# The values of two head pairs: reordered by TensorE transposes instead of a trip through DRAM

## The chip, the core and the metric

The kernel runs on one core of a Trainium2 chip. A core has a matrix engine (TensorE, PE in the profile, with its weight loads listed apart as PEld), a vector engine (VectorE, DVE), a scalar engine (ScalarE, ACT), a general engine (GpSimd, POOL) and a sync engine (SyncE, SP) that here only issues DMA transfers. Each engine works through its own list of instructions in the order in which they were written, and waits on semaphores for the others. PE reads SBUF and writes PSUM, whose eight banks are its scarce resource. The metric is the device time of one execution in microseconds (us).

## What is computed

Attention over blocks comes first, and a bilinear feed-forward layer behind it. The inputs q, k and v are of shape (4, 8, 768, 64): batch, head, position, head dimension. A small 8x8 matrix for each head is normalised by rows and columns five times and then mixes the 8 blocks of k and of v:

```python
P = sort_net                     # (4, 8, 8, 8), normalised five times
k_sorted = einsum('bhij,bhjcd->bhicd', P, k_b)      # blocks of 96 positions
v_sorted = einsum('bhij,bhjcd->bhicd', P, v_b)
scores = q_b @ k_sorted^T / 8                       # inside each block
out    = softmax(scores) @ v_sorted                 # (4, 8, 768, 64)
x = out as (3072, 512)
y = ((x @ w_a) * (x @ w_b)) @ w_out                 # w_a, w_b: 512x1536
```

## The kernel before

**Tiling.** Heads are worked in pairs: batch `b` has pairs `p` = 0 to 3, called (b, p) below. The two heads of a pair lie side by side in the 128 partitions. The feed-forward layer takes one batch at a time, in two halves of 384 positions. Batch 0 uses plain products (`ab_plain`, line 749), batches 1 to 3 a scheme with fewer products over sums of the operands (`ab_strassen`, line 831), and `out_plain` (line 899) multiplies by `w_out`.

**Order.** Every piece of work is an `Op` with an assumed duration, the pieces it depends on, the buffers it takes and gives back, and a rank. `Plan.solve` (line 132) simulates the engines with these assumed durations, picks at each step the piece that can start first (ties by rank), and writes the whole program in that order. So the order on every engine is fixed when the program is built; if a transfer takes longer on the chip than assumed, the engine that needs it waits at that place. Assumed latencies are in the table `LAT`, line 39. If one piece's cost or resources change, the order of all that follows may change a little.

**Stages.** Attention of batch 0 is done first, in half pairs. Then the feed-forward products of batch 0 run on PE (lines 954 to 956) with the attention of batch 1 (lines 958 and 959) put between them, one pair after about three of the 24 products. While this goes on, POOL issues the loads of batch 2 (line 952) and forms sums of weights (`w_sums`, line 769) for the later scheme.

**Values of one pair, by the two routes.** The function `attention` (line 721) calls `q_part`, `mix_part` and `so_part`.

- Through DRAM, where `VDMA(b, p)` is true: `v_tok` (line 534, its products at 537) mixes the pair with 2 products of 384 columns; DVE copies the result from PSUM to the tile `vm`, as 128 x 768 numbers (`v_tok_copy`, line 540, shown under line 250 of the helper `copy`); SP writes `vm` to a DRAM tile `vd` (`v_out`, issue at line 546), waits until this has landed, and reads it back in another order into the tile `vs` (`v_back`, issue at line 550).
- On the chip, where `VDMA` is false: `mix_pe` (line 484, products at 489) mixes with 12 products of 128 columns, so that positions lie along the free dimension; `mix_copy` (line 523) moves the result to the tile `vT`; `v_pe` (line 554, at 559) makes 8 transposes of 128x128, one for each block; `v_copy` (line 562) moves 96 x 1024 numbers to `vs`. The attention of batch 0 uses these steps too, in halves (12 products at line 500, 4 transposes, copies of half the size).

In both routes `o_pe` (line 589, products at 593) multiplies the exponentials `eT` with `vs`, 16 products for a pair. The order of the positions inside a block must be the same for k and v, so `mix_copy` for k writes `kT` in the order that the flag `tc_o` gives; the number of elements is the same. q has its own order and does not depend on the flag.

Buffers: `vs` has 4 slots, `vT` 4, `vm` 2, `v2` (v as loaded) 6. Each pair takes one route only.

In the listing, `sp_dma` adds two pieces: the issue on SP and the transfer. `load` adds a POOL issue and a transfer.

Of the kernel before, what the change touches and what calls it, by code (L numbers as in the profile page):

```python
# [35 lines left out]
class Plan:  # L36
# [12 lines left out]
    def add(self, eng, dur, fn, deps=(), get=(), put=(), rank=0.0, lat=None):  # L49
        alts = dict(eng) if isinstance(eng, (list, tuple)) else {eng: dur}  # L50
        op = Op(alts, fn, deps, list(get), list(put), rank, lat, len(self.ops))
        for key in op.put:
            self.holders[key] = self.holders.get(key, 0) + 1
        self.ops.append(op)
        return op
# [136 lines left out]
STRASSEN_AB = (1, 2, 3)  # L192
STRASSEN_OUT = ()
QDMA = lambda b, p: b >= 3
VDMA = lambda b, p: b >= 1


@with_exitstack
def kernel(
# [284 lines left out]
    def mix_pe(b, p, what):  # L484
        src = buf((what + "2", b, p))
        mix = buf((what + "m", b, p))
        for c in range(NCH):
            for e in range(2):
                nc.tensor.matmul(  # L489
                    mix[e * D:(e + 1) * D, c // 4, c % 4 * P:(c % 4 + 1) * P],  # L490
                    lhsT=src[:, e, c * D:(c + 1) * D],
                    rhs=s_all[:, b * H + 2 * p + e], start=True, stop=True)
# [136 lines left out]
    def mix_part(b, p, rk, split):  # L629

        pair = ("pair",)
        tc_o = VDMA(b, p)
        km = add("PE", 0.46, lambda: mix_pe(b, p, "k"), [k_in[b, p], s_ok[b, p]],
                 get=[("pair", ("km", b, p))], put=[("k2", b, p)], rank=rk)
        ks = []
        for h in ((0, 1) if split else (None,)):
            ks.append(add("ACT", 0.48 if split else 0.8,
                          lambda h=h: mix_copy("ACT", b, p, "k", h, tc_o), [km, o_pads] + ks,
                          get=[("kT", ("kT", b, p))] if not ks else [], put=[("km", b, p)],
                          rank=rk + (0.3 if h == 1 else 0)))  # L640
        if tc_o:
            vm = add("PE", 0.33, lambda: v_tok(b, p), [v_in[b, p], s_ok[b, p]],
                     get=[("pair", ("vm", b, p))], put=[("v2", b, p)], rank=rk)
            vc = add("DVE", 0.95, lambda: v_tok_copy("DVE", b, p), [vm],
                     get=[("vm", ("vb", b, p))], put=[("vm", b, p)], rank=rk)
            vo = sp_dma(0.35, 0.6, lambda: v_out(b, p), [vc], put=[("vb", b, p)], rank=rk)
            vb = sp_dma(0.35, 0.9, lambda: v_back(b, p), [vo, o_pads],
                        get=[("vs", ("vs", b, p))], rank=rk)
            return ks, [vb]
        vm = add("PE", 0.46, lambda: mix_pe(b, p, "v"), [v_in[b, p], s_ok[b, p]],  # L650
                 get=[("pair", ("vm", b, p))], put=[("v2", b, p)], rank=rk + 0.05)
        vs = []
        for h in ((0, 1) if split else (None,)):
            alts = (("DVE", 0.56), ("ACT", 0.48)) if split else (("DVE", 0.95), ("ACT", 0.8))
            op = add(alts, None, None, [vm, o_pads] + vs,
                     get=[("vT", ("vT", b, p))] if not vs else [], put=[("vm", b, p)],
                     rank=rk + (0.3 if h == 1 else 0.05))
            op.fn = lambda h=h, op=op: mix_copy(op.eng, b, p, "v", h, tc_o)
            vs.append(op)
        return ks, vs  # L660
# [20 lines left out]
    def v_part(b, p, h, vsrc, rk):  # L681

        pe = add("PE", 0.28 if h is not None else 0.5, lambda: v_pe(b, p, h), [vsrc, o_ident],
                 get=[("bank", ("vp", b, p, h))], put=[("vT", b, p)], rank=rk)
        alts = (("ACT", 0.6), ("DVE", 0.42)) if h is not None else (("ACT", 1.0), ("DVE", 0.69))
        op = add(alts, None, None, [pe, o_pads, first.get(("v", b, p))],
                 get=[("vs", ("vs", b, p))] if h in (0, None) else [],
                 put=[("vp", b, p, h)], rank=rk)
        first["v", b, p] = op
        op.fn = lambda: v_copy(op.eng, b, p, h)  # L690
        return op
# [29 lines left out]
    def attention(b, p, rk):  # L721
        qd = q_part(b, p, None, rk)
        ks, vs = mix_part(b, p, rk, False)
        if not VDMA(b, p):
            vs = [v_part(b, p, None, vs[0], rk)]
# [337 lines left out]
```

## Time and profile before

| what | value |
|---|---|
| median of 3 runs | 253.11 us (252.26 to 253.12) |
| the profiled execution | 253.12 us |
| its span, first to last instruction | 251.3 us |
| around the span | 1.8 us |
| mean granted TensorE clock | 0.986 |
| PE busy | 237.3 us, 94% of the span |
| DVE busy | 154.4 us, 61% |
| ACT busy | 123.1 us, 49% |
| POOL busy | 115.0 us, 46% |
| issues of `vd` and of `vs` on SP | 12 each, 192 KB each |

Columns as in the profile: "x16" is a number of instructions; a row of the chain of work that ended last has its start, its duration (both in us), and what it was; a row of the DMA issues has the size of one and the time in us from issue to landing; a row of stretches has the busy time of each engine in turn (PE, PEld, DVE, ACT, POOL), then the granted clock, the mean busy share of the 16 DMA engines, and GB/s. `ps` is a tile in PSUM.

### The profile page before, as it was taken

The numbers are of one execution on the slowest core, as the hardware profiler recorded it, in microseconds if no ns is written. First come the engines' busy times: TensorE is split into PE (matmuls) and PEld (weight loads), VectorE is DVE, ScalarE is ACT, GpSimd is POOL, SyncE is SP. The second block draws the span as 40 slices with busy tenths as digits, with TensorE's granted clock in tenths as the row PEclk, the third lists the DMA queues.
The fourth block names the chain that finished last, engine by engine and source line by source line (L and its number), as shares of the span: only waits on it lengthen the run. The fifth ranks groups of instructions, "written<-read, shape, count | busy, mean of one in ns | idle before, by whom it ended". The sixth has DMA issues, their size and how long they took to land.

```text
span 251.3 us, 5639 instructions
## 1 busy us (share of the span) xinstructions
PE 237.3 (94%) x2168; PEld 132.3 (53%) x2168; DVE 154.4 (61%) x355; ACT 123.1 (49%) x239; POOL 115.0 (46%) x127
## 2 busy tenths in 40 slices
PE   7898999993799999999999999999999999999992
PEld 2466766651456445456654445555554455565440
DVE  6656654651348446689889453889885149787120
ACT  3366656453165621576654354867741147664110
POOL 8879999999940002009955110036250004445000
PEclk9999999999589999999999999999999999999999
DMA  5999999999971875534999986600033550000135
GB/s 70 176 202 180 203 202 182 168 202 209 156 136 37 148 195 107 129 87 63 144 142 135 126 205 176 147 3 0 0 65 72 121 120 4 1 0 0 44 83 125
DMA packets 51962, 28.68 MB, mean 114 GB/s; under 512 B 30432, under 2 KB 48864, under 8 KB 51936
## 3 DMA queue, kind: packets, MB, share of 16 engines
q0 software_dynamic: 24112, 14.16, 42.1%
q1 hardware_dynamic: 27824, 14.17, 26.6%
q8 instruction: 17, 0.28, 0.4%
q14 instruction: 9, 0.07, 0.1%
HBM read 30.68 MB, written 8.65 MB: 156 GB/s over the span
## 4 chain that ended last, share of the span: by engine, by line
PE 90%; DMA 5%; POOL 2%; ACT 1%; issue 1%; DVE 0%
PE ps L831 33%; PE ps L899 25%; PE ps L749 13%; PE ps L593 4%; PE ps L578 3%; DMA vs<-vd 3%; DMA q<-in_q_dram 2%; PE ps L473 2%; PE ps L537 2%; PE ps L489 2%; PE ps L500 2%; PE ps L983 1%; PE ps L559 1%; PE ps L612 1%; POOL k L362 1%
## 5 line engine op out<-in xcount | busy, mean ns | idle before, releaser
L306 POOL TENSOR_TENSOR hT<-a,f 128x384 bf16<-128x384 bf16 x34 | 31.1, 920 | 82.0 <-DVE f L306 81.0
L899 PE MATMUL ps<-w_out_sb,hT 128*128 128x512 bf16 x288 | 65.9, 379 | 0.0
L840 ACT COPY f<-ps 128x384 f32<-128x384 f32 x108 | 48.3, 481 | 22.7 <-PE ps L831 18.4
L899 PEld LDWEIGHTS <-hT 128*128 128x128 bf16 x288 | 27.0, 98 | 30.5
L306 DVE TENSOR_TENSOR f<-f,ps 128x384 f32<-128x384 f32 x54 | 29.1, 548 | 6.4 <-PE ps L831 5.0
L306 DVE TENSOR_TENSOR a<-f,ps 128x384 bf16<-128x384 f32 x54 | 29.5, 549 | 5.6 <-PE ps L831 4.2
L306 DVE TENSOR_TENSOR hT<-a,ps 128x384 bf16<-128x384 bf16 x42 | 23.1, 550 | 14.3 <-PE ps L749 7.4
L583 ACT ACTIVATE eT<-ps 96x768 bf16<-96x768 f32 x32 | 25.5, 807 | 11.0 <-PE ps L578 10.6
L248 ACT COPY o<-ps 128x512 f32<-128x512 f32 x14 | 8.1, 585 | 34.7 <-PE ps L899 31.6
L831 PE MATMUL ps<-tx,ws_b 128*128 128x384 bf16 x108 | 25.0, 326 | 0.0
L831 PE MATMUL ps<-tx,ws_a 128*128 128x384 bf16 x108 | 24.7, 327 | 0.0
L755 ACT CAST a<-ps 128x384 bf16<-128x384 f32 x24 | 11.5, 479 | 23.3 <-PE ps L749 19.8
L604 DVE TENSOR_TENSOR xp<-ps,rec 96x512 bf16<-96x512 f32 x32 | 21.5, 680 | 0.4
L250 DVE COPY o<-ps 128x512 f32<-128x512 f32 x10 | 6.9, 690 | 22.4 <-PE ps L899 22.4
L749 PE MATMUL ps<-xT,w_b_sb 128*128 128x384 bf16 x96 | 20.5, 337 | 0.0
L749 PE MATMUL ps<-xT,w_a_sb 128*128 128x384 bf16 x96 | 20.2, 335 | 0.0
L250 DVE CAST vm<-ps 128x768 bf16<-128x768 f32 x12 | 11.5, 956 | 12.3 <-PE ps L537 7.3
L831 PEld LDWEIGHTS <-ws_a 128*128 128x128 bf16 x144 | 13.4, 98 | 10.3 <-ACT f L840 1.6
L831 PEld LDWEIGHTS <-ws_b 128*128 128x128 bf16 x144 | 13.4, 98 | 9.7 <-ACT f L840 1.1
L248 ACT CAST kT<-ps 128x768 bf16<-128x768 f32 (+1 forms) x17 | 11.9, 705 | 13.3 <-PE ps L489 12.2
L593 PE MATMUL ps<-vs,eT 96*128 96x66 bf16 x256 | 12.7, 197 | 5.9 <-DMA vs<-vd 5.9
L831 PE MATMUL ps<-xT,w_b_sb 128*128 128x384 bf16 x72 | 17.4, 326 | 0.1
(88 smaller groups left out, 342.5 us busy)
## 6 DMA issues: line engine op xcount, KB each, us to landing
out_dram<-o SPq DMA_DIRECT2D x48, 128.0 KB, 2.4
k<-in_k_dram POOLq DMA_DIRECT2D x16, 192.0 KB, 5.9
v<-in_v_dram POOLq DMA_DIRECT2D x16, 192.0 KB, 6.2
vd<-vm SPq DMA_DIRECT2D x12, 192.0 KB, 2.4
vs<-vd SPq DMA_DIRECT2D x12, 192.0 KB, 3.2
q<-in_q_dram POOLq DMA_DIRECT2D x16, 96.0 KB, 7.2
w_a_sb<-in_moe_w_a_dram POOLq DMA_DIRECT2D x4, 384.0 KB, 7.3
w_b_sb<-in_moe_w_b_dram POOLq DMA_DIRECT2D x4, 384.0 KB, 8.6
```

The lines of the kernel that those rows point to most:

```text
L248: nc.scalar.copy(out=out, in_=in_)
L250: eng.tensor_copy(out=out, in_=in_)
L306: ENG[eng].tensor_tensor(out=out, in0=in0, in1=in1, op=op)
L578: nc.tensor.matmul(sc[:, e, i * BLK:(i + 1) * BLK], lhsT=kT[e * D:(e + 1) * D, at:at + P], rhs=rhs, start=True, stop=True)
L583: nc.scalar.activation(out=buf(("eT", b, p, h))[:, :, 0:HB], in_=buf(("sc", b, p, h))[0:BLK, :, 0:HB], func=AF.Exp, scale=float(scale))
L593: nc.tensor.matmul(ops_[:, e, i * OW:(i + 1) * OW], lhsT=eT[:, e, i * BLK:i * BLK + P], rhs=vs[:, h * NBH + i, e * OW:(e + 1) * OW], start ...
L604: nc.vector.tensor_tensor(out=_ap(xp, h * NBH * 2 * D, [[NB * 2 * D, BLK], [D, 2], [2 * D, NBH], [1, D]]), in0=_ap(ops_, 2, [[1024, BLK], ...
L749: nc.tensor.matmul(pf[:, 0:HW], lhsT=w_sb[:, kc, m * P:(m + 1) * P], rhs=buf(("xT", b))[:, kc, t * HW:(t + 1) * HW], start=(kc == 0), stop ...
L755: ea = add("ACT", 0.48, lambda: nc.scalar.copy(out=buf(("a", b, t, m)), in_=buf(("pf", b, t, m, "a"))[:, 0:HW]), [pa], get=[("a", ("a", b, ...
L831: nc.tensor.matmul(buf(key)[:, 0:HW], lhsT=lf(j), rhs=rf(j), start=start and j == 0, stop=j == 1, skip_group_check=not start)
L840: return add("ACT", 0.48, lambda: nc.scalar.copy(out=buf((name, b, g, n)), in_=buf(kA)[:, 0:HW]), [dep], get=[("f", (name, b, g, n))], rank=r)
L899: nc.tensor.matmul(po, lhsT=hT[:, t * 2 + m // G, m % G, c * P:(c + 1) * P], rhs=w_out_sb[:, m, :], start=(m == 0), stop=(m == KO - 1), sk ...
```

## The change

```diff
 QDMA = lambda b, p: b >= 3
-VDMA = lambda b, p: b >= 1
+VDMA = lambda b, p: 4 * b + p >= 6
```

`4 * b + p` counts the pairs from 0 to 15. Before, pairs 4 to 15 (all of batches 1, 2 and 3) went through DRAM. Now pairs 6 to 15 do, and pairs 4 and 5, that is (1,0) and (1,1), take the route on the chip. `VDMA` is asked at two places: in `mix_part` (`tc_o`, line 632), where it chooses the route and the order of positions in `kT`, and in `attention` (line 724), where the transposes and their copy are added:

```python
        if not VDMA(b, p):
            vs = [v_part(b, p, None, vs[0], rk)]
```

`v_part` (line 681) adds the 8 transposes, in one PSUM bank, and one copy to `vs`, on ACT or DVE as the plan prefers. Everything else in the source is the same; the program's order is worked out anew.

## The prediction

> **What bounds the kernel now.** I read the page from the top: the busy shares, then the 40 slices (6.28 us each), then the chain of work that ended last.
>
> ```profile
> PE   7898999993799999999999999999999999999992
> PEclk9999999999589999999999999999999999999999
> DMA  5999999999971875534999986600033550000135
> PE 90%; DMA 5%; POOL 2%; ACT 1%; issue 1%; DVE 0%
> ```
>
> TensorE is busy in nearly every slice and makes up 90% of the chain, so time falls only where PE idles, runs at a low clock, or does less. After the start one hole is left: the tenth and eleventh slices of PE ("3", "7"), followed by a dip of the clock ("5", "8"). The DMA row shows the sixteen engines full until just there. The view of waits names the hole, and the chain in order of time gives its place.
>
> ```profile
> PE ps L593 <- DMA vs<-vd: 5.9, 1, 5.9
> ```
>
> ```profile
> 49.34 0.43 PE ps L537 x2
> 49.77 1.30 PE ps L749 x8
> ...
> 57.02 7.42 DMA vs<-vd
> ...
> 64.48 1.04 PE ps L593 x16
> 65.53 2.56 PE ps L749 x8
> ...
> 69.50 0.75 PE ps L537 x2
> ...
> 79.17 0.26 PE ps L593 x8
> ```
>
> It is a single wait, by the products with `vs` at line 593. PE mixed the values of pair (1,0) at 49.34 (line 537); its products with `vs` stand 8.8 us of PE work later in the order (49.77 to 58.6), and `vs` had landed only at 64.44. The issues on SP, in order of time, show why, and tell which pair it is: the first write of `vd` and the first read back in the whole program.
>
> ```profile
> 50.80 0.36 SPq L546 DMA_DIRECT2D vd<-vm  x1
> 57.02 0.33 SPq L550 DMA_DIRECT2D vs<-vd  x1
> ```
>
> The write took from 50.80 to 57.02, the read back from 57.02 to 64.44: 13.6 us for a trip for which the order left 8.8 minus the copy. The later pairs take the same trip; by the view of waits PE waited for none of them.
>
> The price of the hole is more than the wait. Three stretches, with the clock behind the five engines:
>
> ```profile
> 48.55:81.36 32.81, 26.92 (x311) 16.50 (x312) 15.61 (x31) 15.29 (x25) 23.13 (x20) 0.90 0.89 150
> ...
> 58.60:64.48 5.88, 0.00 (x0) 0.00 (x0) 0.01 (x1) 0.56 (x2) 5.86 (x6) 0.93 1.11 192
> 64.48:70.46 5.98, 5.97 (x52) 3.66 (x52) 2.32 (x6) 1.98 (x3) 5.91 (x7) 0.50 1.12 166
> ```
>
> PE does nothing from 58.60 to 64.48, and then works for 5.98 us at clock 0.50. The chain agrees: 8 products of line 749 take 2.56 us at 65.53 and 1.30 us at 49.77. Half of 5.97 is 2.98; as some of the last rows overlap the return of the clock, I take 2.9. The hole costs 5.9 + 2.9 = 8.8 us.
>
> **The change, part by part.**
>
> *Removed: the wait, -5.9, and the slow stretch, -2.9.* Pair (1,0) no longer needs a transfer. Its new chain is: mix, copy to `vT`, 8 transposes, copy to `vs`. The nearest rows for the copies:
>
> ```profile
> L250 DVE CAST vm<-ps 128x768 bf16<-128x768 f32 x12 | 11.5, 956 | 12.3 <-PE ps L537 7.3
> ...
> L250 DVE COPY vs<-ps 96x512 bf16<-96x512 bf16 x5 | 2.1, 419 | 1.6 <-PE ps L559 1.6
> ```
>
> The copy to `vT` has the elements of the `vm` copy, 0.96 us; that to `vs` is two of the 0.42 us halves, 0.84. With 0.7 for the transposes that is 2.5 us, and about 3 with hand-overs, against 8.8 us of PE work between. So `vs` of (1,0) is ready near 53, and of (1,1) near 59; neither wait can be late next unless DVE falls far behind.
>
> *Added on PE: +1.1.* Per pair, the mix of v changes from 2 products (0.43 in the chain) to 12 (line 489), and 8 transposes come (line 559; only groups of 4 exist, in batch 0):
>
> ```profile
> 16.63 0.33 PE ps L559 x4
> ...
> 27.46 0.23 PE ps L559 x4
> ...
> 93.31 0.46 PE ps L489 x12
> ```
>
> A mix costs 0.34 (its share within a run of attention work) to 0.46, the transposes 2 x 0.23 = 0.46 to 2 x 0.33 = 0.66. Per pair that is between 0.34 + 0.46 - 0.43 = +0.37 and 0.46 + 0.66 - 0.43 = +0.69, for two pairs +0.7 to +1.4. Nothing hides it, since PE is the bound; less than nothing is excluded, as work is only added. I take the middle, 1.1.
>
> [...]
>
> *Added on DVE and ACT: 0.* Per pair one copy more, 0.84 us if DVE does it. In the stretch 48.55 to 81.36, DVE is busy 15.61 and ACT 15.29 us. Without the hole that stretch shrinks to about 32.8 - 8.8 + 1.1 = 25.1 us, in which DVE would have 17.3 (69%). That cover is enough on average; a local pile-up, where a PSUM bank comes free late, would cost PE a few tenths, and at the very most the 1.7 us of the added copies. I take 0.
>
> *Removed on SP and the DMA engines.* Four issues leave SP, and four transfers of 192 KB leave the DMA engines, all in the full stretch. SP then has nothing ahead of the trip of (1,2), where before it stood behind two waits for landings. The order of `kT` positions changes, not the number of elements: 0. POOL's loads and weight sums have no part in the route; POOL is busy 5.86 of 5.88 us in the hole, so the loads go on being paced by POOL's own list at their old times, while PE comes some 7 us earlier.
>
> *Moved: the trip of (1,2), now the first, +0.3.* This is the wait that could take the place of the old one. In PE order its mix stood at 69.50 and its products with `vs` at 79.17. With 8.8 us less and 1.1 more, the products are due at 71.5. Between the mix and its issue of `vd` lie 1.5 us (49.34 to 50.80). From the mix at 69.50 - 8.6 + 1.1, moved on by up to 0.5 because the products of (1,1) can now come before it, the issue follows at 63.5 to 64. So `vd` and `vs` may take about 7.4 us together. What such transfers took, by the DMA issues of short stretches around 51, 57, 65 and 71:
>
> ```profile
> vd<-vm SPq DMA_DIRECT2D x1, 192.0 KB, 6.1
> ...
> vs<-vd SPq DMA_DIRECT2D x1, 192.0 KB, 7.4
> ...
> vs<-vd SPq DMA_DIRECT2D x1, 192.0 KB, 4.2
> ...
> vd<-vm SPq DMA_DIRECT2D x1, 192.0 KB, 2.2
> ```
>
> And loads by POOL, in stretches around 49 and 63:
>
> ```profile
> k<-in_k_dram POOLq DMA_DIRECT2D x1, 192.0 KB, 12.4
> ...
> v<-in_v_dram POOLq DMA_DIRECT2D x1, 192.0 KB, 4.1
> ```
>
> The backlog is gone by 63: a load takes 4.1 us there, not 12.4. So the trip starting near 64 is nearest to the rows at 65 and 71: `vd` about 3, `vs` 4.2, together 7.2, just in time. From 2.2 + 4.2 = 6.4 (no wait) to 6.1 + 7.4 = 13.5 (a wait of 6.1) everything is possible; I take 0.3. Pair (1,3) and batch 2 follow when the loads have ended, and their data are used far later than their landing.
>
> *Sum.* 251.3 - 5.9 - 2.9 + 1.1 + 0.3 = 243.9 us of span; with the 1.8 us around it, 245.7. The profiled execution (253.12) is the median of the runs (253.11), so no correction.
>
> **The rivals.**
>
> 1. *The wait moves to (1,2), in part.* For it: the trip has no slack, and the order may be worked out so that loads come earlier. Against it: four transfers less, and the backlog gone by 63. With `vd` as at 51 and `vs` as at 65, 6.1 + 4.2 = 10.3, PE waits 2.9 instead of 0.3: 248.3. The clock fell at about 63.7 (0.93 over 5.88 us is 0.8 us at half), 5 us after PE stopped, so such a wait would not bring the clock down. [...]
> 2. *Slower: the whole hole moves to (1,2).* If its trip is as slow as that of (1,0), 13.5 us, PE waits 6.1, over the 5 us, and the clock falls again, 2.9: 251.3 - 8.8 + 1.1 + 6.1 + 2.9 + 1.8 = 254.4. It decides from a trip of about 12 us on, where new wait, clock and added work match the 8.8. For it: the first trip took that long. Against it: the latencies fall through the stretch.
> [...]
> 4. *DVE or ACT in the way.* The added copies hold PSUM banks and PE stops now and then, up to the 1.7 us: 247.4.
> 5. *The change does nothing to the end.* The new order puts other pieces so that PE loses elsewhere what it gains, 252.5 to 254. By the view of waits PE has no other wait of a microsecond once the loads of batch 0 are in, so nothing shows where.
>
> **How the numbers follow.** Forecast 0.62; an order still a little better than that 0.05; rival 1 0.16; rival 2 0.05; rival 3 0.03; rival 4 0.06; rival 5 0.03. Predicted is the forecast's 245.7. Its own bounds are 245.0 (PE +0.7, no wait) to 247; the range goes down to 244.5 for a better order, and up to 249.5 for most of rival 1 and for rivals 3 and 4; what it leaves out is rivals 2 and 5 and the worst of rival 1, about 0.13. Faster by over 0.5% (about what a measurement of this kernel can tell from no change) is below 251.8: 0.91. Within 0.5% falls most of rival 5 and the worst of rival 1, 0.04; slower is rival 2, 0.05.
>
> **What would show it.** Right: no wait of line 593 on `vs` near 58, clock 1.00 in the slices that had 5 and 8, 16 more rows of line 559 with 58 to 83 ns each, ten issues each of `vd` and `vs`, the first `vd` near 64. Wrong: a wait of line 593 on `vs` near 71 with a length of more than a microsecond (rivals 1 and 2), PE idle behind ACT or DVE between 50 and 75 (rival 4), or groups of 8 transposes over 1 us (rival 3).

## The result, and the profile after

| | before | after |
|---|---|---|
| median | 252.69 us (251.88 to 253.12, 4 runs) | 245.32 us (244.20 to 245.70, 4 runs) |
| profiled execution, span | 253.12, 251.3 us | 245.06, 243.3 us |
| granted clock, mean | 0.986 | 1.0 |

The ratio is 0.9705, with a 95% interval of 0.9661 to 0.9749. The forecast was 245.7 us, and 243.9 us of span.

The slices of the page after, in 40 parts of 6.08 us:

```profile
PE   6998999999989999999999999999999999999992
PEclk9999999999999999999999999999999999999999
DMA  5999999999965683619998867200035450000135
```

The hole in the PE row and the dip in the clock are gone. What is left of a hole is the "8" in the twelfth slice. Where the products with `vs` of the three pairs stand now is seen in the timeline of PE (start, duration, line; in brackets idle time before, with its releaser):

```profile
49.56 0.53 PE L489 MATMUL ps<-s_all,v 128*64 128x128 bf16 x12
51.12 0.61 PE L559 MATMUL ps<-ident,vT 128*128 128x128 bf16 x8
52.87 0.67 PE L593 MATMUL ps<-vs,eT 96*128 96x66 bf16 x16
...
56.32 0.53 PE L489 MATMUL ps<-s_all,v 128*64 128x128 bf16 x12
57.98 0.62 PE L559 MATMUL ps<-ident,vT 128*128 128x128 bf16 x8
59.74 0.74 PE L593 MATMUL ps<-vs,eT 96*128 96x66 bf16 x16
...
71.96 0.41 PE L593 MATMUL ps<-vs,eT 96*128 96x66 bf16 x8 [0.78 <-ACT eT L583]
```

Pairs (1,0) and (1,1) are mixed, transposed and multiplied within 4.2 us each, without a wait. Pair (1,2) waits 0.78 us. The row names ACT, but the trip says otherwise. Its issues on SP, and what the two transfers took:

```profile
64.03 0.36 SPq L546 DMA_DIRECT2D vd<-vm  x1
69.27 0.33 SPq L550 DMA_DIRECT2D vs<-vd  x1
```

```profile
vd<-vm SPq DMA_DIRECT2D x1, 192.0 KB, 5.2
...
vs<-vd SPq DMA_DIRECT2D x1, 192.0 KB, 2.6
```

69.27 + 2.6 is 71.9, the moment at which PE goes on; ACT finished an exponential of a later pair at the same time, 71.96, by chance. In another execution of the same kernel (after_again below) PE starts these products in the middle of that exponential and waits for nothing, because `vs` had landed at 69.19 + 2.6 = 71.8:

```profile
71.59 1.51 ACT L583 ACTIVATE eT<-ps 96x768 bf16<-96x768 f32 x2
72.16 0.42 PE L593 MATMUL ps<-vs,eT 96*128 96x66 bf16 x8
```

The two stages around the change, in the changed kernel: from the first transposes of q of (1,0) to the end of the batch-0 products, and from there to the last product.

```profile
48.01:73.94 25.93, 25.15 (x347) 16.20 (x348) 14.86 (x30) 17.29 (x28) 23.29 (x21) 1.00 1.01 160
73.94:238.70 164.76, 163.92 (x1224) 88.83 (x1224) 105.05 (x209) 82.49 (x165) 51.15 (x57) 1.00 0.51 90
```

The first stage took 32.9 us before and takes 25.9 us; the second took 165.1 us before and takes 164.7 (the last product ends at 238.67).

### The profile page after: what moved, and what is told of

Same layout as the page of the kernel before. It is cut to its first block, busy times and chain, and to the rows that moved or that the text cites. A ratio compares the mean times of both kernels' runs of the same rounds, so it can differ in the third digit from the quotient of the medians.

```text
span 243.3 us, 5723 instructions
## 1 busy us (share of the span) xinstructions
PE 233.7 (96%) x2204; PEld 132.4 (54%) x2204; DVE 150.1 (62%) x348; ACT 125.3 (52%) x243; POOL 119.6 (49%) x132
## 3 DMA queue, kind: packets, MB, share of 16 engines
q1 hardware_dynamic: 25968, 13.38, 25.7%
## 4 chain that ended last, share of the span: by engine, by line
PE 67%; ACT 1%; DVE 1%; issue 0%; ACTq 0%; DVEq 0%
PE ps L831 33%; PE ps L899 26%; PE ps L593 2%; PE ps L578 2%; PE ps L489 1%; PE ps L537 1%; PE ps L473 1%; PE ps L749 1%; ACT f L840 0%; DVE xp L604 0%; ACT o L248 0%; DVE a L306 0%; DVE rec L599 0%; ACTq L840 0%; DVEq L306 0%
## 5 line engine op out<-in xcount | busy, mean ns | idle before, releaser
L306 POOL TENSOR_TENSOR hT<-a,f 128x384 bf16<-128x384 bf16 x39 | 35.5, 918 | 78.1 <-DVE f L306 56.3
L583 ACT ACTIVATE eT<-ps 96x768 bf16<-96x768 f32 x32 | 24.9, 806 | 17.2 <-PE ps L578 16.9
L248 ACT COPY o<-ps 128x512 f32<-128x512 f32 x15 | 8.8, 585 | 36.3 <-PE ps L899 36.3
L831 PE MATMUL ps<-tx,ws_a 128*128 128x384 bf16 x108 | 25.2, 326 | 0.2 <-ACT f L840 0.2
L749 PE MATMUL ps<-xT,w_a_sb 128*128 128x384 bf16 x96 | 19.6, 327 | 0.0
L749 PE MATMUL ps<-xT,w_b_sb 128*128 128x384 bf16 x96 | 19.6, 326 | 0.0
L250 DVE COPY o<-ps 128x512 f32<-128x512 f32 x9 | 6.2, 691 | 20.8 <-PE ps L899 20.7
L831 PE MATMUL ps<-xT,w_b_sb 128*128 128x384 bf16 x72 | 17.6, 326 | 0.3 <-DVE xp L604 0.2
L831 PE MATMUL ps<-xT,w_a_sb 128*128 128x384 bf16 x72 | 17.5, 326 | 0.0
L831 PEld LDWEIGHTS <-w_b_sb 128*128 128x128 bf16 x108 | 10.4, 98 | 7.9 <-DVE xp L604 0.7
L831 PEld LDWEIGHTS <-w_a_sb 128*128 128x128 bf16 x108 | 10.3, 98 | 7.9 <-ACT f L840 0.6
```

What stands on the lines that cost most here:

```text
L248: nc.scalar.copy(out=out, in_=in_)
L250: eng.tensor_copy(out=out, in_=in_)
L306: ENG[eng].tensor_tensor(out=out, in0=in0, in1=in1, op=op)
L583: nc.scalar.activation(out=buf(("eT", b, p, h))[:, :, 0:HB], in_=buf(("sc", b, p, h))[0:BLK, :, 0:HB], func=AF.Exp, scale=float(scale))
L749: nc.tensor.matmul(pf[:, 0:HW], lhsT=w_sb[:, kc, m * P:(m + 1) * P], rhs=buf(("xT", b))[:, kc, t * HW:(t + 1) * HW], start=(kc == 0), stop ...
L831: nc.tensor.matmul(buf(key)[:, 0:HW], lhsT=lf(j), rhs=rf(j), start=start and j == 0, stop=j == 1, skip_group_check=not start)
```

## The experiments

Ratios are to the kernel before, measured beside each, with 95% intervals. The table gives what the trace of each profiled execution shows; stage 1 and stage 2 are the two stretches above, cut at the same instructions, and "in 1" is the time in stage 1 in which no matrix product ran. A new order can move products of line 593 over the cut, about 0.5 us for each 16: compared with the kernel before, stage 1 lacks 32 of them in e5, 16 in e6 and 10 in e2, and has 16 more in e8. The last column adds up, over all 504 products of line 831, the time from one start to the next (a dash: not added up).

| kernel | median | ratio | stage 1 | in 1 | stage 2 | line 831 |
|---|---|---|---|---|---|---|
| before | 252.7 | 1 | 32.9 | 5.9 | 165.1 | 83.9 |
| after | 245.3 | 0.9705 | 25.9 | 0.8 | 164.7 | 84.1 |
| after_again | 245.1 | 0.9721 (0.9689 to 0.9754) | 25.0 | 0 | 164.7 | 84.1 |
| e1, only (1,0) moved | 249.7 | 0.9888 (0.9832 to 0.9945) | 27.5 | 3.0 | 166.1 | - |
| e10, e1 once more | 249.9 | 0.9892 (0.9838 to 0.9945) | 27.1 | 2.6 | 166.1 | - |
| e2, only (1,1) moved | 253.1 | 1.0011 (0.9969 to 1.0053) | 32.2 | 6.9 | 166.0 | - |
| e3, (1,2) moved too | 245.9 | 0.9767 (0.9729 to 0.9804) | 25.7 | 0 | 164.7 | 83.8 |
| e4, products in the hole | 250.5 | 0.9924 (0.9892 to 0.9956) | 29.9 | 0.1 | 165.1 | - |
| e5, plan told the trip | 247.1 | 0.9810 (0.9764 to 0.9856) | 23.0 | 0 | 167.9 | 85.4 |
| e6, after, plan told | 246.0 | 0.9753 (0.9719 to 0.9786) | 24.5 | 0 | 167.2 | 84.0 |
| e7, transposes five times | 248.0 | 0.9823 (0.9774 to 0.9871) | 28.6 | 0 | 164.7 | - |
| e8, all pairs moved | 259.0 | 1.0262 (1.0200 to 1.0323) | 27.0 | 0 | 177.6 | - |
| e9, idle trips, early | 250.9 | 0.9975 (0.9938 to 1.0012) | 25.0 | 0 | 167.6 | 85.5 |
| e11, idle trips in place | 250.0 | 0.9869 (0.9826 to 0.9912) | 27.4 | 2.3 | 167.6 | 85.5 |

### Which pair, and is it the wait: e1, e10 and e2

```diff
-VDMA = lambda b, p: b >= 1
+VDMA = lambda b, p: 4 * b + p >= 5                  # e1, e10
+VDMA = lambda b, p: b >= 1 and (b, p) != (1, 1)     # e2
```

> Only pair (1,0) takes the route on the chip; (1,1) and all later pairs go through DRAM. Theory (the gain is the one wait of (1,0) and the slow clock behind it; each pair on the chip costs PE about 0.55 us): the hole of 8.8 us is gone, 0.55 us is added, and the trip of (1,1), now the first, starts near 57 in full DMA engines: about 10 us where its place in the order allows 7.6, so PE waits about 2.4 us (0.5 to 4.2) at line 593 and the clock stays. Time 252.7 - 8.8 + 0.55 + 2.4 = 246.9 (245.0 to 248.7). Rival (the gain comes from taking traffic off the full DMA engines, in proportion to the pairs moved): half of the gain of the change, about 249.

> Only pair (1,1) takes the route on the chip; (1,0) goes through DRAM as before. Theory: the wait of (1,0) stays nearly whole, its trip 12 to 13.6 us, so PE waits 4 to 6 us near 59; whether the clock falls depends on being above or below 5 us. Time 250 to 253.3, likeliest 252. Rival (less traffic is what counts, or any pair moved is as good as another): about 249, and PE waits under 2 us.

The views of waits, of e1 and of e2:

```profile
PE ps L593 <- DMA vs<-vd: 3.0, 2, 2.6
```

```profile
PE ps L593 <- DMA vs<-vd: 6.9, 1, 6.9
```

Moving (1,1) alone gains nothing: (1,0) still waits, 6.9 us, longer than the 4 to 6 expected, and a pair's worth of PE work is added. Moving (1,0) alone ends the long wait, and (1,1) becomes the first trip, with a wait of 2.6 us against the 2.4 expected. So the gain belongs to the wait of (1,0), not to any pair moved. But e1's median is 1.0 us above the top of its range. Its profiled execution was the fastest, 248.0, so the kernel was run once more for a second profile.

> The kernel with only (1,0) on the chip once more, for a second profile: its median was 249.7, 2.8 above what was expected, while its profiled execution (248.0) was the fastest of five and had a wait of 2.6 us for (1,1). Theory: in the slower executions the trip of (1,1) ends later, PE waits 4 to 5 us near 66 and the clock falls behind it; a profile at 249.5 or more shows a slow stretch between 66 and 76. Rival: the slow stretch lies elsewhere, ahead of 45 us, and has nothing to do with the pair.

The second profile (249.1 us) has the same wait, and a slow stretch in another place, as the rival said:

```profile
PE ps L593 <- DMA vs<-vd: 2.3, 1, 2.3
```

```profile
20.40:23.90 3.50, 3.50 (x65) 2.68 (x60) 1.62 (x4) 1.77 (x4) 3.50 (x6) 0.52 1.22 182
```

That stretch lies in batch 0 and costs 1.7 us. The mean clock of the first profile, 0.996 against 0.990, leaves no room for one of that length. The profile of e5, in which (1,0) goes through DRAM, has one like it (clock 0.76 from 23 to 30 us), so it does not belong to the pair. Stage 2 is also 1.4 us longer than in the changed kernel. The stretch is not the whole of the miss: one execution at a mean clock of 1.0 still took 249.3 us. The rest of e1's miss is open.

### Does the clock follow the idle time: e4

```diff
+        if (b, p, h) == (1, 0, 0):
+            for n in range(27):
+                nc.tensor.matmul(ops_[:, n % 2, :], lhsT=warm_sb[:, 0:P], rhs=warm_sb,
+                                 start=True, stop=True)
         for i in range(NBH):        # o_pe, in the kernel before
```

> The kernel before with 27 products of 512 columns of zeros, whose result is overwritten, put on PE directly ahead of the products that wait for vs of (1,0). They take 27 x 0.216 = 5.8 us, as long as the wait, so PE is busy while vs is on its way, and the wait itself is not shortened. Theory (the slow 6 us behind the hole come from PE having been idle): the clock stays at 1.00 and the time falls by 2.9 us to about 249.8. Rival (the low clock has another cause, or its cost is hidden behind POOL and the DMAs): no change, 252.7.

Timeline and stretches of e4: the products of zeros fill the wait, and the products behind it run at full clock (line 753 is line 749 of the kernel before; two groups of four start 0.65 us apart, where the kernel before took 2.56 for eight).

```profile
60.33 5.78 PE L593 MATMUL ps<-warm_sb 128*128 128x512 bf16 x26
65.94 0.67 PE L597 MATMUL ps<-vs,eT 96*128 96x66 bf16 x16
66.45 0.81 PE L753 MATMUL ps<-xT,w_b_sb 128*128 128x384 bf16 x4
67.10 0.81 PE L753 MATMUL ps<-xT,w_a_sb 128*128 128x384 bf16 x4
```

```profile
60.00:66.00 6.00, 5.95 (x30) 2.73 (x30) 0.29 (x1) 0.84 (x2) 5.96 (x6) 1.00 0.97 164
66.00:72.00 6.00, 6.00 (x83) 3.83 (x82) 3.77 (x8) 3.38 (x6) 5.87 (x6) 1.00 1.10 156
```

Stage 1 is 29.9 us against 32.9: the slow clock was worth 2.96 us in the trace, 2.9 in the forecast. The medians differ by 2.1, less than that. Some executions of the kernel before have a mean clock of 0.990 instead of 0.984: with all the rest at 1.0 that is 5 us at half clock instead of 8, an estimate from these means and the spans of 249.0 and 250.5 us; no profile of such an execution shows where. The profiled execution of e4 itself has a low clock elsewhere: its mean is 0.988, with 1.00 from 60 to 72 us, and outside the two stages it takes 1.8 us more than the kernel before.

### What a transpose costs: e7

```diff
-        for i in range(n):
+        for i in [j for j in range(n) for _ in range(5 if h is None else 1)]:
```

> The changed kernel with each of the 16 added transposes made five times into the same place, 64 more transposes, order otherwise the same. Theory (a transpose in a group costs PE 55 to 77 ns): 64 x 0.055 to 0.077 = 3.5 to 4.9 us more than the changed kernel's 245.3, so 248.8 to 250.2, clock 1.00 throughout. [...]

The groups of transposes in the timeline of e7:

```profile
50.98 2.40 PE L559 MATMUL ps<-ident,vT 128*128 128x128 bf16 x40
...
59.62 2.41 PE L559 MATMUL ps<-ident,vT 128*128 128x128 bf16 x40
```

40 take 2.40 us, 8 took 0.61: 56 ns for each of the 32 more. The time rose by 2.7 us, 0.8 below the expected range. In the trace PE now comes to the products of (1,2) after `vs` has landed, so the wait of 0.8 us of the changed kernel's first profile is gone. Against after_again, whose trace has no such wait either, stage 1 rose from 25.0 to 28.6 us, which is 64 x 56 ns. The mean granted clock of this trace was 1.0.

### Further along the line: e3 and e8

```diff
+VDMA = lambda b, p: 4 * b + p >= 7    # e3
+VDMA = lambda b, p: False             # e8
```

> The changed kernel again, beside the three that follow: 245.3 (244.2 to 245.7), PE waits about 0.8 us for vs of (1,2).

> Pair (1,2) takes the route on the chip too; the first trip is that of (1,3). Theory: the wait of 0.8 us of (1,2) goes, 0.55 us of PE work comes: 245.1 (244.3 to 245.9), the same as the changed kernel within what can be measured. Rival (every pair off DRAM helps by itself): about 1 us or more faster, 244.

> All twelve pairs of batches 1 to 3 take the route on the chip, no trip through DRAM at all. Theory (where no wait is removed, each pair moved only adds PE work, 0.53 us as the changed kernel's stage showed): ten pairs more than in the changed kernel, + 5.3 - 0.3: 250 (249 to 251.5). Rival (DRAM trips cost something everywhere): 245 or less.

The changed kernel came out as before. A third pair changes nothing that can be measured: where the wait of 0.8 us goes, about 0.6 us of PE work comes in its place. In e8 the PE work is as expected (the trace has 5.1 us more of it than in the changed kernel), but the time is 7.5 us above the range. Two new waits stand in stage 2, each with a stretch at half clock behind it:

```profile
PE ps L559 <- DVE o L250: 3.6, 1, 3.6
PE ps L489 <- DVE xp L604: 3.0, 1, 3.0
```

They come to 6.6 us, and the slow stretches to 3.4 more. Both waits lie behind the transposes of `xp` by DMA, as the chain has it:

```profile
80.69 11.84 DMA xT<-xp
```

The transposes run beside loads here. The new order issues the first load of the last batch at 71.51 us, where the changed kernel issues it at 107.22. The POOL rows of e8 and of the changed kernel, and the transposes of `xp`, e8's issued from 76 to 84 us and the changed kernel's from 73 to 84:

```profile
71.51 0.74 POOL L362 DMA_DIRECT2D k<-in_k_dram  x1
107.22 0.76 POOL L362 DMA_DIRECT2D k<-in_k_dram  x1
```

```profile
xT<-xp SPq DMA_TRANSPOSE x3, 11.8
xT<-xp SPq DMA_TRANSPOSE x3, 2.9
```

So e8 does not price the route alone: its new order also moved these loads. No run takes the loads away from the transposes, so that they are the cause is argued, not shown.

### Only the place in the order: e5 and e6

```diff
+    LATE = {(1, 0): (4.0, 4.5), (1, 1): (4.5, 1.5), (1, 2): (2.5, 0.0)}   # us, vd and vs
-        return add("DQ", work, None, [i], put=put, rank=rank - 100.0, lat=1.5)
+        return add("DQ", work, None, [i], put=put, rank=rank - 100.0, lat=1.5 + late)
```

> The kernel before, all pairs of batch 1 through DRAM, but the plan is told that the trips of (1,0), (1,1) and (1,2) take 8.5, 6.0 and 2.5 us longer than it assumed, so it puts other products ahead of those that need vs. Theory (the loss is the place of the waiting products in PE's order, not the route): no wait at line 593, no slow clock, and none of the added PE work: 252.7 - 8.8 = 243.9 (243.2 to 245.5). Rival (the route itself costs: the engines are late anyway and the wait shows up elsewhere): 247 or more.

> The changed kernel with the plan told that the trip of (1,2) takes 2.5 us longer than assumed. Theory: the wait of 0.8 us goes and nothing is added: 244.5 (243.8 to 245.5). Rival (the wait of 0.8 us was covered by slack behind it): 245.3.

In e5 all pairs go through DRAM, and PE waits for none: the products of (1,0) stand at 67.85, and `vs`, issued at 58.48, had landed 5.8 us later, at 64.3. Rows of its timeline and its stretch:

```profile
67.85 0.68 PE L595 MATMUL ps<-vs,eT 96*128 96x66 bf16 x16
```

```profile
49.00:80.00 31.00, 31.00 (x397) 18.79 (x396) 19.46 (x37) 17.52 (x29) 22.60 (x20) 1.00 1.07 182
```

So the hole can be closed without a transpose, as the theory says. But the time, 247.1, lies above the range of 243.2 to 245.5 and just on the rival's side. The new order loses elsewhere part of what it saves: both stages together are 190.9 us, where the kernel before without hole and slow clock would have 189.1. PE idles 1.6 us in stage 2, in waits of at most 0.4 us, where the kernel before idles 0.1; line 831 takes 1.5 us more. Another 1.6 us lie ahead of stage 1, where this execution has a slow stretch in batch 0 (clock 0.76 from 23 to 30 us). e6 closes the wait of 0.8 us and has 1.0 us of waits for `vs` of later pairs in stage 2 instead; its 246.0 lies 0.5 above its range. Neither beats the changed kernel.

### Traffic or wait: e9 and e11

> The changed kernel, with the trips of (1,0) and (1,1) made all the same: zeros are written to DRAM and read back into a place that nobody reads, at the times and in the sizes of the kernel before, so that SP and the DMA engines keep the whole traffic and only PE no longer waits for it. Theory (the gain is the wait of PE, not the traffic): nearly all of the gain stays; the trip of (1,2) starts about 1.4 us later on SP and ends near 72 to 73, so PE waits 0.5 to 2 us: 246.5 (245.3 to 248). Rival (the relief of SP and of the DMA engines is half of the gain or more): 249 or more.

That kernel missed its aim. Nothing tied the idle trips to the pairs, so SP issued them as soon as it could, the first at 12.54 us, into the loads of batch 0, and the added clearing of `vm` on POOL held up loads too. PE lost time ahead of stage 1 (stage 1 begins at 51.7 us instead of 48.0); stage 1 itself is as in the changed kernel. So its time, though on the rival's side, says nothing about traffic beside the pairs. The second form ties them to `vT`:

```diff
+        vo = sp_dma(0.35, 0.6, lambda: idle_out(b, p), [vs[0]], put=[("vT", b, p)], rank=rk)
+        sp_dma(0.35, 0.9, lambda: idle_back(b, p), [vo],
+               get=[("o", ("idle", b, p))], put=[("idle", b, p)], rank=rk)
```

> The changed kernel, with the trips of (1,0) and (1,1) made all the same, and now tied to the copies of these pairs to vT, so that they run near 51 to 64 and 58 to 69 as in the kernel before (in the kernel e9 nothing tied them down, and they ran between 12 and 30): the first 768 columns of vT go to DRAM and come back into a place that nobody reads. SP and the DMA engines keep the traffic of the kernel before, only PE does not wait for it. Theory (the gain is the wait of PE and the clock behind it, not the traffic): nearly all of the gain stays; the trip of (1,2) starts about 1.4 us later and PE waits 0.5 to 2 us for it near 72, clock 1.00: 246.5 (245.3 to 248). Rival (the relief of SP and of the DMA engines is half of the gain or more): 249 or more.

The chain of e11 in order of time, at the trip of (1,2):

```profile
64.66 5.25 DMA vd<-vm
...
69.97 4.46 DMA vs<-vd
...
74.47 0.67 PE ps L602 x16
```

It starts 0.6 us later than in the changed kernel and takes 9.8 us instead of 7.9; PE waits 2.25 us. In stage 1 that is what the theory said, 0.5 to 2 us, and a little more: 27.4 us against 25.0 and 25.9, so stage 1 keeps 5.5 of the 7.0 us it had gained. Of the later start, 0.4 us is that stage 1 itself begins at 48.41 instead of 48.01. The longer trip is all in `vs`, 4.5 us instead of 2.6, and beside it run two loads that POOL issued late:

```profile
68.66 0.74 POOL L362 DMA_DIRECT2D v<-in_v_dram  x1
69.39 0.72 POOL L406 DMA_DIRECT2D q<-in_q_dram  x1
```

In the changed kernel the last of these loads was issued at 65.78, ahead of `vs`. So the 1.5 to 2.4 us that stage 1 loses are the traffic of the idle trips and later loads together; the two were not told apart.

The time as a whole fell on the rival's side, 250.0. The rest is stage 2, 2.9 us longer, with 1.4 us of it in line 831. That is not the traffic of the idle trips: in e9 they had ended by 38 us and in e11 by 70, both ahead of stage 2, and both kernels have the same 167.6 us there, with the same order of products on PE, which is not that of the changed kernel. So this part of the loss goes with the new order.

## Why the prediction was right, step by step

- **The wait, -5.9.** Right. e2 and e5 show that it hung on (1,0) alone and on where its products stand.
- **The slow clock, -2.9.** Right; e4 took it away by itself and measured 2.96 in the trace.
- **PE work, +1.1.** Right: PE is busy 25.15 us in stage 1, against 32.9 - 5.9 - 3.0 = 24.0. A mix costs 0.46, eight transposes 0.45 from start to start.
- **DVE and ACT, 0.** Right in stage 1. The copies to `vT` went to ACT, those to `vs` took 0.69 us on DVE, not 0.84.
- **The trip of (1,2), +0.3.** The mechanism was right, the issue came at 64.03 as forecast (the 8.6 in that sum should be 8.4, as at 69.50 only 2.5 us of the slow clock's cost had passed, which gives 63.7 to 64.2), but the split was not: `vd` took 5.2 and not 3, `vs` 2.6 and not 4.2. The sum 7.9 gave a wait of 0.78 in one execution, and 6.6 gave none in another.
- **Loads at their old times.** Wrong: POOL's order was worked out anew as well, and the last load was issued at 65.78, not 69.41. In e11, with the last loads at 68.66 and 69.39, `vd` took 5.25 and `vs` 4.5, and PE waited 2.25 us. So that the wait came out near 0.3 is in part luck: `vd` was slower than forecast, and `vs`, behind loads that ended early, was faster.
- **Removed traffic, 0.** It had no term of its own. e11 gives at most 1.5 to 2.4 us for it, later loads included. That the backlog is gone by 63 did not hold for `vd`, which took 5.2 us from 64.03.
- **The clock behind a shorter wait (rival 1), only above 5 us.** Wrong, without effect on the sum: in e2 the clock fell 3.3 us after PE had stopped, and in e8 after waits of 3.0 and 3.6 us. A wait of 3 us for (1,2) could have cost the slow clock too. Rival 2's trip of 12 us, a wait of 4.6, counted the slow clock already below the 5 us that rival 1 asks for. No run shows the cost with which the worst of rival 1 is counted, nor the pace behind rival 3 and so behind a part of the range up to 249.5: in e8 the half clock behind each wait lasted 3.4 us, a loss of 1.7, and the groups of eight transposes took 0.61 and 0.62 us.
- **Everything behind, 0.** It came out at -0.4 us, but a new order alone can move stage 2 by more: by 1.8 us in e5 and 2.0 in e6, without the products that went behind the cut, and by 2.9 in e9 and e11. Rival 5 deserved more than 0.03.

Of the 8.0 us that the span lost, 7.0 are stage 1 and 0.4 stage 2; 0.6 lie ahead of and behind the two, which no step of mine had, and that is within what executions of one kernel differ by (242.4 to 243.9 us of span).

## What to carry to other kernels

When one engine is busy over nine tenths of the span, price a wait of that engine at its length plus the slow clock that the trace shows behind it (here 5.9 + 2.9 us; behind the 2.25 us of e11 there was none), and ask first which single piece of work waits, and where it stands in that engine's order; moving another, equal piece gains nothing (e2, a ratio of 1.0011). A plan with one latency for every such trip does not know the queue: here trips took 6.1 + 7.4 us among the loads, and 2.2 + 2.6 behind them. Where a program's order is worked out as a whole, any local change rolls the dice for everything behind it, here by up to 3 us, and by 10 in e8, so measure the stage and the whole apart.

## What the runs showed of the hardware that was not expected

The clock fell after waits of PE far shorter than the 5 us that I had read from the profile before. In e2 it fell 3.3 us after PE had stopped:

```profile
58.41:61.70 3.29, 0.00 (x1) 0.00 (x0) 0.08 (x1) 0.32 (x1) 3.27 (x3) 1.00 1.30 212
61.70:65.30 3.60, 0.00 (x0) 0.00 (x0) 0.00 (x0) 0.00 (x0) 3.60 (x5) 0.50 1.02 149
```

In e8 the stretches around its two waits (3.0 and 3.6 us without a product) show the same:

```profile
80.70:83.72 3.02, 0.01 (x3) 0.01 (x2) 0.69 (x1) 1.78 (x3) 0.70 (x1) 1.00 1.80 154
83.72:87.12 3.40, 3.40 (x26) 1.85 (x27) 0.56 (x2) 0.80 (x1) 0.71 (x1) 0.50 1.61 121
92.02:95.59 3.57, 0.00 (x0) 0.03 (x1) 2.81 (x6) 0.00 (x0) 0.00 (x0) 1.00 0.84 112
95.59:97.37 1.78, 1.78 (x38) 1.44 (x39) 1.10 (x3) 0.55 (x1) 0.00 (x0) 1.00 0.36 83
97.37:100.78 3.41, 3.41 (x10) 1.21 (x9) 1.08 (x2) 0.94 (x2) 0.00 (x0) 0.50 0.40 92
```

After the first wait the clock is at half for 3.40 us from the moment PE resumes; after the second it falls only 1.8 us after PE has resumed, and again for 3.41 us. The two falls lie 13.65 us apart. The waits of 2.3 and 2.25 us in e10 and e11 had none behind them: the clock of e10 is 1.00 from 60 to 90 us, and the mean of e11 is 1.0.
